# Fused pooled attention and top-1 MoE: two homes for the left operands, one flag for each engine, branches issued ahead of the seven products

## Chip, cores and metric

The kernel runs on one core of a Trainium2 chip. The metric is the device time of one execution in microseconds (us). The engines are TensorE (PE, with its weight loads as PEld), VectorE (DVE), ScalarE (ACT), GpSimd (POOL) and SyncE (SP, which only issues DMAs here).

## What is computed

Attention over keys and values that are averaged in groups of 8, then a mixture of experts in which each of 4608 tokens goes to the one expert with the highest gate.

```python
q, k, v: (8, 8, 576, 64)            # batch, heads, sequence, head size
k_p, v_p = mean of k, v over groups of 8 positions
attn = softmax(q @ k_p.T / 8) @ v_p
x = attn as (4608, 512)             # N tokens, D
logits = x @ w_gate + modality_bias[modality_id]      # 8 experts
e_idx, gate_w = argmax, softmax value there
out[n] = gate_w[n] * (relu(x[n] @ w1[e]) @ w2[e])     # w1: (8, 512, 1024), w2: (8, 1024, 512)
```

## The kernel before

Attention, gating and routing fill the first quarter of the time and are the same in both kernels. Then tokens are sorted by expert into slots of 256 tokens (SLOT). Slots 0 to 17 (NSTAT = 18) always run, one after the other, and the last of them is widened by 128 tokens where that is enough for all. Tokens of one expert fill slots in a row, so that a slot has either the expert of the slot before it or a new one; a flag of 0 or 1 in `meta` says which.

The hidden size of 1024 is worked on in eight blocks f of 128 rows (NF = 8), two blocks making a pair p (0 to 3, with g = 2p). Float32 operands are split in a high and a low part, and each product is made of three: high by high, high by low, low by high. The weights' split parts stand in `hl[f]` (first 512 columns w1, the others w2), each made from a float32 copy `raw[f]`.

For a pair, `hidden_sums` (L195) makes the first products: 24 matmuls (L201) into one PSUM bank `hp`, both chunks (one a block) in the same bank. From slot 3 (FIRST_SEVEN) to slot 16 the second product is done in Strassen's manner, with seven products in place of eight. `first_seven` (L218) applies the relu on ScalarE (L221, L222), VectorE makes sums of the halves (L223 to L225), and `rest` splits them into the left operands `left` (casts on ScalarE, L228 and L230, the low parts on VectorE, L229 and L231). `left` has one home, which every pair overwrites. `seven` (L242) then multiplies, 21 matmuls (L248), with blocks of w2 and with sums of them (`ext[p]`, the "x" pieces) into four PSUM banks that gather over the four pairs. `evac_seven` (L1464) empties these banks at the start of the next slot: ScalarE copies four products with the gate as scale (L1472), GpSimd combines two and two (L1473, L1474), VectorE makes six combinations (L1477), of which products 0 and 1 lie in bank 0.

The order of issue in a slot s is that of `pairs` (L1567), on every engine's queue: for pair 0 the evacuation of the slot before; for pairs 1 to 3 the first products of this pair, the seven products of the pair before, `rest`, `misc`, and `step_done`; at the end, the first products of pair 0 of the next slot, the seven products of pair 3, `rest` and `step_done(4)`. `misc` (L1602) holds the preparation of tokens: gathers, scaling on GpSimd (L326), a write to DRAM (`scr`, L329), a read of it in another order (`y`, L343), transposes on VectorE (L353), and the splits L1399 (ScalarE) and L1404 (VectorE).

`step_done` calls `turn`, which renews the weights for the next slot piece by piece: steps 1 to 4 within slot s, 5 to 7 in the first three steps of slot s + 1. In a step GpSimd makes sums in place in `raw` (SUMS, L253 and L260), ScalarE casts the high parts (L279) and VectorE subtracts for the low parts (L283) of the pieces in PIECES, and SP issues the loads of `raw` of the pairs in FREED for the slot after (L130, L135). Sums and pieces stand in a branch (`changed`, L1496) that is passed over where the expert stays. A branch is issued on all three of ScalarE, VectorE and GpSimd, whichever of them has work in it. For slot 3 the pieces are made without a branch. The last slot but one, 16, has a renewal of its own (`renew_last`, L1507). The only lists that set the order are these:

```python
PIECES = {2: [(0, "e"), (0, "o")], 3: [(1, "e"), (1, "o")], 4: [(0, "x"), (2, "e")], 5: [(2, "o"), (1, "x")],
          6: [(3, "e"), (3, "o"), (2, "x")], 7: [(3, "x")]}
FREED = {4: [0], 5: [1], 6: [2], 7: [3]}
```

## Time and profile before

| | |
|---|---|
| median of 3 runs | 742.31 us (740.21 to 743.71) |
| the profiled execution's own time | 742.09 us |
| its span, first to last instruction | 740.3 us |
| mean granted clock of PE | 0.916 |
| PE busy | 609.7 us, 82% of the span |
| VectorE, GpSimd, ScalarE busy | 446.5 (60%), 311.2 (42%), 306.2 us (41%) |

A slot is told here from the first products of its pair 1 to those of the next slot's. By that, slot 2 goes from 215.74 to 237.93 us, slot 3 to 268.45, slots 4 to 7 to 390.65, 8 and 9 to 465.53, 10 to 12 to 557.62 (11 from 496.33 to 527.10), 13 and 14 to 632.82, 15 to 663.72 and 16 to 696.94. Slots 8, 9, 13 and 14 are those in which pieces are made for a new expert. Busy time of PE is from modelled ends, and a granted clock of 1 is 2.4 GHz, of 0.5 1.2 GHz.

### The profile page before, as it was taken

Reading aid. Unit: us, or ns where it says so; the run is one execution under the profiler, and the core shown is the slowest. Engines: PE = TensorE matmul, PEld = TensorE weight load, DVE = VectorE, ACT = ScalarE, POOL = GpSimd, SP = SyncE. Lnnn points to the kernel's source line nnn. Section 1 sums busy time; section 2 is a strip of 40 time slices with the busy share of each in tenths; the row PEclk is TensorE's granted clock in tenths of the full one; section 3 lists DMA queues with packets and bytes.
Section 4 is the critical chain, followed back from the end, with each engine's and each line's share of the span. In section 5 each row is a group of like instructions: output and inputs, shape, how many; then the busy total and the mean of one; then the engine's idle time right before and its main releaser. Section 6 shows DMA issues by size and latency. Waiting matters only on the chain. (4 is left out here: it accounts for less than half of the span.)

```text
span 740.3 us, 15072 instructions
## 1 busy us (share of the span) xinstructions
PE 609.7 (82%) x4503; PEld 572.8 (77%) x4503; DVE 446.5 (60%) x1009; ACT 306.2 (41%) x702; POOL 311.2 (42%) x438
## 2 busy tenths in 40 slices
PE   5999999999999687786887767786887767885797
PEld 5898999989999687686876767786877757784785
DVE  6878887887665674635536665635536676546321
ACT  3776778963223432432424344422324343423310
POOL 7799686500318623413134644314134655422011
PEclk9999999999999989988989777988989777988889
DMA  9999998431552213112135331112135431223201
GB/s 268 322 291 370 311 336 256 150 111 61 173 171 88 86 44 102 65 53 94 37 101 165 124 111 59 59 59 94 37 101 165 121 93 64 66 86 101 58 31 44
DMA packets 83253, 94.91 MB, mean 128 GB/s; under 512 B 18191, under 2 KB 56591, under 8 KB 83152
## 3 DMA queue, kind: packets, MB, share of 16 engines
q1 hardware_dynamic: 77232, 74.34, 32.3%
q0 software_dynamic: 5920, 19.44, 8.2%
q8 instruction: 37, 0.61, 0.4%
q14 instruction: 64, 0.52, 0.2%
HBM read 113.63 MB, written 28.62 MB: 192 GB/s over the span
## 5 line engine op out<-in xcount | busy, mean ns | idle before, releaser
L201 PE MATMUL hp<-xhl,hl 128*128 128x256 f32 x1536 | 222.3, 304 | 74.0 <-ACTq L1498 44.4
L201 PEld LDWEIGHTS hp<-xhl,hl 128*128 128x128 f32 x1536 | 209.5, 211 | 82.5 <-ACTq L1498 48.8
L248 PE MATMUL op<-hl,after_arow 128*128 128x256 f32 x504 | 83.1, 314 | 26.7 <-DVE ob L1477 26.0
L248 PEld LDWEIGHTS op<-hl,after_arow 128*128 128x128 f32 x504 | 75.6, 222 | 31.1 <-issue 17.3
L223 DVE TENSOR_TENSOR hs<-hs 128x256 f32<-128x256 f32 x56 | 26.5, 473 | 117.6 <-ACT hs L222 116.8
L1473 POOL TENSOR_TENSOR part<-part 128x256 f32<-128x256 f32 x14 | 10.2, 726 | 169.1 <-ACT part L1472 169.1
L221 ACT ACTIVATE hs<-hp 128x256 f32<-128x256 f32 x56 | 21.5, 384 | 142.3 <-PE hp L201 140.8
L231 DVE TENSOR_TENSOR left<-hs,left 128x512 fp32r<-128x512 f32 x56 | 41.4, 738 | 43.2 <-ACT left L230 24.9
L248 PE MATMUL op<-hx,left 128*128 128x256 f32 x378 | 54.8, 291 | 5.4 <-ACT hx L279 4.0
L228 ACT CAST after_arow<-hs 128x384 fp32r<-128x384 f32 x56 | 28.8, 514 | 71.1 <-PE op L248 44.9
L1488 POOL DMA_INDIRECT out_dram<-ob,sidx x28 | 31.9, 1138 | 56.7 <-DMA out_dram<-ob,sidx 29.4
L248 PEld LDWEIGHTS op<-hx,left 128*128 128x128 f32 x378 | 50.8, 202 | 6.1 <-ACT hx L279 4.2
L326 POOL TENSOR_TENSOR xg<-xg 128x256 f32<-128x256 f32 x56 | 47.5, 870 | 17.5 <-DMA xg<-xs,gidx 17.4
L230 ACT CAST left<-hs 128x512 fp32r<-128x512 f32 x56 | 34.7, 620 | 46.3 <-PE op L248 36.6
L792 PE MATMUL av<-vw,pt 128*128 128x146 f32 (+1 forms) x320 | 48.9, 292 | 0.7 <-DVE xb L825 0.6
L148 POOL DMA_INDIRECT xg<-xs,gidx x36 | 38.4, 1067 | 17.6 <-issue 8.0
L792 PEld LDWEIGHTS av<-vw,pt 128*128 128x128 f32 (+1 forms) x320 | 39.6, 180 | 2.5 <-ACT pt L776 0.8
L1477 DVE SCALAR_TENSOR_TENSOR ob<-op,gc,part 128x256 f32<-128x256 f32 x56 | 26.9, 480 | 19.4 <-POOL part L1473 11.9
L229 DVE TENSOR_TENSOR after_arow<-hs,after_arow 128x384 fp32r<-128x384 f32 x56 | 31.6, 565 | 10.3 <-ACT after_arow L228 7.2
L728 PE MATMUL sc<-kt,qt 128*128 128x144 f32 x256 | 37.0, 288 | 0.7 <-ACT qt L709 0.7
L283 DVE TENSOR_TENSOR hl<-raw,hl 128x256 fp32r<-128x256 f32 (+1 forms) x32 | 29.4, 951 | 9.8 <-ACT hl L279 9.3
L728 PEld LDWEIGHTS sc<-kt,qt 128*128 128x128 f32 x256 | 33.2, 190 | 1.2 <-ACT qt L709 0.6
(298 smaller groups left out, 1220.5 us busy)
## 6 DMA issues: line engine op xcount, KB each, us to landing
raw<-in_moe_w_dram SPq DMA_DIRECT2D x248, 256.0 KB
scr<-xg SPq DMA_DIRECT2D x35, 256.0 KB
xs<-xb SPq DMA_DIRECT2D x16, 528.0 KB
k<-in_k_dram SPq DMA_DIRECT2D x7, 1024.0 KB
v<-in_v_dram SPq DMA_DIRECT2D x7, 1024.0 KB
q<-in_q_dram SPq DMA_DIRECT2D x7, 1024.0 KB
y<-scr SPq DMA_DIRECT2D x108, 64.0 KB
v<-in_v_dram SPq DMA_DIRECT2D x16, 128.0 KB
```

What stands on the lines that cost most here:

```text
L148: nc.gpsimd.indirect_dma_start(out=x, out_offset=None, in_=xs[0:rows, :], in_offset=IndirectOffsetOnAxis(idx[:, col:col + 1].bitcast(U32), 0),
L201: nc.tensor.matmul(ph[:, c], hl[g + c][:, w, d * P:(d + 1) * P], ab[:, d, x, 0:SLOT], start=(n == 0 and d == 0), stop=(n == 2 and d == ND ...
L228: nc.scalar.copy(left[0][0], hs[:, 1:4])
L229: nc.vector.tensor_sub(left[0][1], hs[:, 1:4], left[0][0].bitcast(F32))
L230: nc.scalar.copy(left[1][0], hs[:, 4:8])
L231: nc.vector.tensor_sub(left[1][1], hs[:, 4:8], left[1][0].bitcast(F32))
L248: nc.tensor.matmul(at_, left[a][x][:, i], right(p, w, n), start=(p == 0 and k == 0 and n % 2 == 0), stop=(p == NF // 2 - 1 and k == 2 and ...
L283: nc.vector.tensor_sub(lo, src, hi.bitcast(F32))
L326: nc.gpsimd.tensor_tensor(xo, xi, f[:, :, a].to_broadcast([P, ND, 2, QUAD]), op=ALU.mult)
L728: nc.tensor.matmul(dst, qt[:, i, :], kt[b % NB][:, :, h * SPL:(h + 1) * SPL], start=True, stop=True)
L792: nc.tensor.matmul(av[hs, u, 2 * VC * gg:2 * VC * (gg + 1)], pt[:, c, hs], vw[y][:, c].rearrange("p a x -> p (a x)"), start=(gg == 0), sto ...
L1488: nc.gpsimd.indirect_dma_start(out=out[:, :], out_offset=IndirectOffsetOnAxis(idx.bitcast(U32), 0), in_=ob, in_offset=None, bounds_check=N ...
```

## The change

The left operands get a second home (`lefts1`, in the place of a tile that is free in slots 3 to 15), and pairs take turns between the two; so `rest` runs at once after the sums, up to slot 15. In slot 16 there is one home, and `rest` stays behind the seven products. `step_done` is called ahead of the seven products and of `misc`. Each branch is on one engine, with a flag in a register of that engine. The pieces (2, "o"), (3, "e"), (3, "o") and all "x" pieces are made one step earlier, the sums of pairs 2 and 3 likewise, and the loads of `raw` too. The two chunks of a pair lie in two PSUM banks, and pairs take turns between the halves of a bank. The evacuation takes products 0 and 1 first, in VectorE's combinations without GpSimd, whose two instructions come last. Some tiles (`ye`) are used in slots 2 and 3 alone. The diff, without its unchanged lines:

```diff
+ACT, DVE, POOL_ = mybir.EngineType.Activation, mybir.EngineType.DVE, mybir.EngineType.Pool
...
     def hidden_sums(g, ab):
-        ph = hp[(g // 2) % 2].rearrange("p (c t) -> p c t", c=2)
+        h_ = (g // 2) % 2 * SLOT
+        ph = hp2[:, :, h_:h_ + SLOT]
...
-        return lambda: None
-    def first_seven(g, ab):
+    def first_seven(q, g, ab):
...
+        l0, l1 = left[q, g // 2] = lefts[g // 2 % 2 if q < NSTAT - 2 else 0]
...
         def rest():
-            nc.scalar.copy(left[0][0], hs[:, 1:4])
-            nc.vector.tensor_sub(left[0][1], hs[:, 1:4], left[0][0].bitcast(F32))
-            nc.scalar.copy(left[1][0], hs[:, 4:8])
-            nc.vector.tensor_sub(left[1][1], hs[:, 4:8], left[1][0].bitcast(F32))
+            nc.scalar.copy(l0[0], hs[:, 1:4])
+            nc.scalar.copy(l1[0], hs[:, 4:8])
+            nc.vector.tensor_sub(l0[1], hs[:, 1:4], l0[0].bitcast(F32))
+            nc.vector.tensor_sub(l1[1], hs[:, 4:8], l1[0].bitcast(F32))
+        if q < NSTAT - 2:
+            rest()
+            return lambda: None
...
-    def seven(p):
+    def seven(q, p):
...
-                nc.tensor.matmul(at_, left[a][x][:, i], right(p, w, n),
+                nc.tensor.matmul(at_, left[q, p][a][x][:, i], right(p, w, n),
...
-        elif tt == 0 and s <= EARLY_SLOTS:
+        elif tt == 0 and s < FIRST_SEVEN + 1:
...
     def blocks_turn(s, tt):
...
-        elif s <= EARLY_SLOTS:
+        elif s < FIRST_SEVEN + 1:
...
-    hp = [ps_hp.tile([P, 512], F32, name=f"hp{i}") for i in range(2)]
+    hp2 = ps_hp.tile([P, 2, 512], F32, name="hp")
+    hp = [hp2[:, i] for i in range(2)]
...
-    left = [None, second_left[:, 0:8 * P].rearrange("p (z n t) -> p z n t", z=2, n=4)]
-    left[1] = [left[1][:, z] for z in range(2)]
+    lefts, left = [[None, [second_left[:, 4 * P * z:4 * P * (z + 1)].rearrange("p (n t) -> p n t", n=4) for z in range(2)]]], {}
     def take_rows():
...
-        left[0] = [a[:, z] for z in range(2)]
+        lefts[0][0] = [a[:, z] for z in range(2)]
+        b = mp.tile([P, 2 * ND * (SLOT + P)], F32R, tag="xw", name="lefts1")[:, P - 16:]
+        lefts.append([b[:, k * 6 * P:k * 6 * P + 2 * n * P].rearrange("p (z n t) -> p z n t", z=2, n=n) for k, n in ((0, 3), (1, 4))])
+        lefts[1] = [[x[:, z] for z in range(2)] for x in lefts[1]]
...
-    PIECES = {2: [(0, "e"), (0, "o")], 3: [(1, "e"), (1, "o")], 4: [(0, "x"), (2, "e")], 5: [(2, "o"), (1, "x")],
-              6: [(3, "e"), (3, "o"), (2, "x")], 7: [(3, "x")]}
+    PIECES = {2: [(0, "e"), (0, "o")], 3: [(1, "e"), (1, "o"), (0, "x")], 4: [(2, "e"), (2, "o"), (1, "x")],
+              5: [(3, "e"), (3, "o"), (2, "x")], 6: [(3, "x")]}
...
-            4: [(more_sums_of, 1), (sums_of, 3)], 6: [(more_sums_of, 2)], 7: [(more_sums_of, 3)]}
-    FREED = {4: [0], 5: [1], 6: [2], 7: [3]}
+            4: [(more_sums_of, 1), (sums_of, 3)], 5: [(more_sums_of, 2)], 6: [(more_sums_of, 3)]}
+    FREED = {3: [0], 4: [1], 5: [2], 6: [3]}
     def slot_flag(s):
-        flags[s] = nc.values_load(meta[0:1, 2 + NSLOT + s:3 + NSLOT + s],
-                                  engines=[mybir.EngineType.Activation, mybir.EngineType.DVE, mybir.EngineType.Pool], min_val=0, max_val=1,
-                                  skip_runtime_bounds_check_because="a comparison's result")
+        for e in (mybir.EngineType.Activation, mybir.EngineType.DVE, mybir.EngineType.Pool):
+            flags[s, e] = nc.values_load(meta[0:1, 2 + NSLOT + s:3 + NSLOT + s], engines=[e], min_val=0, max_val=1,
+                                         skip_runtime_bounds_check_because="a comparison's result")
     def part(s):
...
-            for n, dst, g in ((1, e2, g0), (2, e5, g1), (4, e6, g0), (5, e7, g1)):
+            low, high = slice(0, H2), slice(H2, D)
+            for n, dst, g in ((2, e5, g1), (1, e2, g0), (4, e6, g0), (5, e7, g1)):
...
-            nc.gpsimd.tensor_sub(e6, e6, e2)
-            nc.gpsimd.tensor_add(e7, e7, e5)
             def combine(out_, n, g, b, minus=False):
...
-            combine(obs[1][:, H2:D], 0, g1, e5)
-            combine(obs[0][:, H2:D], 0, g0, e6)
-            combine(obs[0][:, H2:D], 3, g0, obs[0][:, H2:D])
-            combine(obs[1][:, 0:H2], 6, g1, e7, minus=True)
-            combine(obs[1][:, 0:H2], 3, g1, obs[1][:, 0:H2])
-            combine(obs[0][:, 0:H2], 6, g0, e2)
+            combine(obs[1][:, high], 0, g1, e5)
+            combine(obs[0][:, high], 0, g0, e2, minus=True)
+            combine(obs[0][:, high], 3, g0, obs[0][:, high])
+            combine(obs[1][:, low], 3, g1, e5, minus=True)
+            combine(obs[1][:, low], 6, g1, obs[1][:, low])
+            combine(obs[0][:, low], 6, g0, e2)
+            nc.gpsimd.tensor_add(obs[0][:, high], obs[0][:, high], e6)
+            nc.gpsimd.tensor_sub(obs[1][:, low], obs[1][:, low], e7)
...
-        def changed(fn, q=s + 1):
-            with tc.If(flags[q] > 0, preferred_fallthrough_block=False):
+        def changed(eng, fn, q=s + 1):
+            with tc.If(flags[q, eng] > 0, preferred_fallthrough_block=False):
...
         def renew(f):
...
-                lag.append(lambda: (changed(lambda: split_hi(f)), changed(lambda: split_lo(f, nc.vector))))
+                lag.append(lambda: (changed(ACT, lambda: split_hi(f)), changed(DVE, lambda: split_lo(f, nc.vector))))
         def renew_last(p):
...
-                for do in (halve_hi, halve_lo):
+                for eng, do in ((ACT, halve_hi), (DVE, halve_lo)):
                     def all_of(do=do, part=part):
...
-                        changed(all_of)
+                        changed(eng, all_of)
...
-                work.append(lambda: [fn(p) for fn, p in SUMS[step]])
-            for do in (halve_hi, halve_lo):
+                work.append((POOL_, lambda: [fn(p) for fn, p in SUMS[step]]))
+            for eng, do in ((ACT, halve_hi), (DVE, halve_lo)):
                 def all_of(do=do):
...
-                    work.append(all_of)
-            for fn in work:
+                    work.append((eng, all_of))
+            for eng, fn in work:
...
-                    changed(fn, q + 1)
+                    changed(eng, fn, q + 1)
...
         def step_done(step):
+            if step < 4:
+                turn(s - 1, step + 4)
...
-            if step < 4:
-                turn(s - 1, step + 4)
+            elif step > 1:
+                renew_last(step - 2)
             if s == FIRST_SEVEN - 2:
...
         def first_of(q, g):
-            return (first_seven if FIRST_SEVEN <= q < NSTAT - 1 else first_pair)(g, tokens_of(q))
+            if FIRST_SEVEN <= q < NSTAT - 1:
+                return first_seven(q, g, tokens_of(q))
+            first_pair(g, tokens_of(q))
+            return lambda: None
         def second_pair(p):
...
-                seven(p)
+                seven(s, p)
...
                 if g:
...
+                    step_done(g // 2)
...
-                        seven(g // 2 - 1)
+                        seven(s, g // 2 - 1)
...
-                    if s == NSTAT - 2:
-                        renew_last(g // 2 - 1)
-                    step_done(g // 2)
...
-                    if s == NSTAT - 2:
-                        xw[0] = mp.tile([P, ND, 2, SLOT + P], F32R, tag="xw", name="xw")
...
+                    if s == NSTAT - 2:
+                        xw[0] = mp.tile([P, ND, 2, SLOT + P], F32R, tag="xw", name="xw")
...
+                step_done(4)
...
-                step_done(4)
         def misc(f, later):
...
         def close(first_of_next=first_next):
...
-                seven(NF // 2 - 1)
+                renew_last(NF // 2 - 2)
+                seven(s, NF // 2 - 1)
...
```

## Rows read from the trace of the kernel before

**Rows 1.** Busy time of each engine by stretches (us from the span's start): slot 2, slot 3, slots 4 to 7, 8 and 9, 10 to 12, 11 alone, 13 and 14, 15, 16. Behind each engine's busy time stand its instructions; PEclk is the granted clock.

```profile
215.74:237.93 22.19, 22.19 (x148) 20.31 (x146) 10.65 (x22) 5.31 (x12) 16.94 (x22) 1.00 0.30 98
237.93:268.45 30.52, 24.41 (x181) 23.55 (x180) 21.06 (x46) 13.15 (x27) 13.76 (x14) 0.89 0.22 70
268.45:390.65 122.20, 95.86 (x722) 92.05 (x721) 61.76 (x142) 39.52 (x88) 36.97 (x40) 0.92 0.22 71
390.65:465.53 74.88, 54.48 (x363) 52.36 (x361) 47.86 (x77) 30.27 (x56) 38.37 (x40) 0.82 0.36 113
465.53:557.62 92.09, 73.55 (x543) 70.75 (x541) 44.78 (x97) 29.65 (x66) 27.22 (x30) 0.89 0.22 70
496.33:527.10 30.77, 24.75 (x182) 23.81 (x181) 14.93 (x33) 9.88 (x22) 9.00 (x10) 0.89 0.22 70
557.62:632.82 75.20, 53.90 (x363) 51.81 (x361) 48.80 (x77) 30.37 (x56) 38.20 (x40) 0.82 0.36 111
632.82:663.72 30.90, 24.35 (x183) 23.41 (x181) 15.39 (x33) 9.88 (x22) 11.20 (x13) 0.89 0.27 87
663.72:696.94 33.22, 23.39 (x171) 22.33 (x169) 16.73 (x39) 11.64 (x27) 4.66 (x5) 0.90 0.28 79
```

In each row: stretch, its length, then PE, PEld, DVE, ACT, POOL, the granted clock, the DMA engines' share and GB/s.

**Rows 2.** PE's timeline in slot 11: start, time, instructions in a row, and in brackets the idle time before them and what ended it.

```profile
500.30 0.93 PE L248 MATMUL op<-hl,after_arow 128*128 128x256 f32 x6 [0.97 <-DVE ob L1477]
501.73 0.59 PE L248 MATMUL op<-hl,after_arow 128*128 128x256 f32 x3 [0.51 <-DVE ob L1477]
...
506.41 1.63 PE L201 MATMUL hp<-xhl,hl 128*128 128x256 f32 x12 [1.31 <-ACTq L1498]
...
512.33 1.21 PE L201 MATMUL hp<-xhl,hl 128*128 128x256 f32 x8 [1.91 <-ACTq L1498]
514.86 3.78 PE L201 MATMUL hp<-xhl,hl 128*128 128x256 f32 x16 [1.32 <-DVEq L1498]
...
521.80 2.99 PE L201 MATMUL hp<-xhl,hl 128*128 128x256 f32 x24
524.63 1.23 PE L248 MATMUL op<-hl,after_arow 128*128 128x256 f32 x9
...
527.10 2.89 PE L201 MATMUL hp<-xhl,hl 128*128 128x256 f32 x24
```

**Rows 3.** The view of waits over the whole run: who waited for whom, us in total, times, the longest. ACTq and DVEq L1498 are the branches on those engines.

```profile
ACT after_arow L228 <- PE op L248: 44.9, 25, 4.2
PE hp L201 <- ACTq L1498: 44.4, 22, 4.7
ACT left L230 <- PE op L248: 36.6, 43, 2.1
PE op L248 <- DVE ob L1477: 26.0, 24, 4.9
PE hp L201 <- DVEq L1498: 16.1, 10, 2.1
PE hp L201 <- ACT hl L279: 10.3, 4, 3.3
```

**Rows 4.** The timeline of VectorE and of ScalarE in slot 11 (columns as in rows 2), VectorE first.

```profile
499.67 0.48 DVE L1477 SCALAR_TENSOR_TENSOR ob<-op,gc,part 128x256 f32<-128x256 f32 x1 [0.76 <-POOL part L1473]
...
511.04 1.14 DVE L231 TENSOR_TENSOR left<-hs,left 128x512 fp32r<-128x512 f32 x1 [0.59 <-ACT left L230]
...
512.77 1.03 DVE L1404 TENSOR_TENSOR xhl<-yt,xhl 128x512 fp32r<-128x512 f32 x1
...
526.20 0.28 DVE L225 TENSOR_TENSOR hs<-hs 128x128 f32<-128x128 f32 x1
527.88 0.69 DVE L231 TENSOR_TENSOR left<-hs,left 128x512 fp32r<-128x512 f32 x1 [0.74 <-ACTq L1498]
...
497.56 1.57 ACT L1472 ACTIVATE part<-op,gc 128x256 f32<-128x256 f32 x4 [0.48 <-ACTq L1498]
...
510.39 0.62 ACT L230 CAST left<-hs 128x512 fp32r<-128x512 f32 x1 [0.53 <-PE op L248]
...
524.83 0.39 ACT L221 ACTIVATE hs<-hp 128x256 f32<-128x256 f32 x1 [2.28 <-PE hp L201]
```

**Rows 5.** Groups of instructions by line and shape in slots 8 and 9: count, busy us and mean ns of one, idle time before them and what ended it.

```profile
L283 DVE TENSOR_TENSOR hl<-raw,hl 128x1024 fp32r<-128x1024 f32 x8 | 10.7, 1369 | 2.5 <-ACT hl L279 2.4 <-issue 0.2
L279 ACT CAST hl<-raw 128x1024 fp32r<-128x1024 f32 x8 | 8.1, 1042 | 1.1 <-issue 1.1
L256 POOL TENSOR_TENSOR raw<-raw,raw 128x256 f32<-128x256 f32 x4 | 4.5, 1132 | 6.9 <-DMA raw<-in_moe_w_dram 6.9
L263 POOL TENSOR_TENSOR raw<-raw,raw 128x256 f32<-128x256 f32 x4 | 3.7, 922 | 6.6 <-DVE hl L283 4.2 <-issue 1.4 <-DMA scr<-xg 1.0
L283 DVE TENSOR_TENSOR hx<-raw,hx 128x768 fp32r<-128x768 f32 x3 | 3.4, 1133 | 0.1
L279 ACT CAST hx<-raw 128x768 fp32r<-128x768 f32 x3 | 2.5, 828 | 0.0
```

**Rows 6.** PE's timeline in slot 9: the seven products of pair 0, with the idle time before them.

```profile
433.17 2.41 PE L248 MATMUL op<-hl,after_arow 128*128 128x256 f32 x9 [4.61 <-DVE ob L1477]
```

**Rows 7.** The branches' line: engine, instruction, count, shortest, median and longest ns, first and last start.

```profile
L1498 ACTq COMPARE_BRANCH  x448: 34/38/50, 246.2 to 700.2; - x150
```

**Rows 8.** SP's timeline in slot 11: the eight reads of y, from the first issue to the end of the last.

```profile
516.42 3.67 SPq L343 DMA_DIRECT2D y<-scr  x8
```

## The prediction, made before the changed kernel was run

> **What bounds the kernel now.** I read the stretches first, one slot each [rows 1]. Slot 2, still with plain second products, is the measure: 22.19 us long, PE busy for 22.19 of them, clock 1.00. Every slot with seven products should be shorter, as four block pairs of 24 + 21 matmuls are 180. In slot 11 the undisturbed part shows their price: 24 first products take 2.83 us from start to start (521.80 to 524.63), 21 of the seven products 2.47 (524.63 to 527.10) [rows 2]. A step is 5.30 us, a slot 21.2. It takes 30.77, with PE at a granted clock of 0.89 [rows 1].
>
> The same timeline says where the 9.6 us go [rows 2]. PE stands for 0.97 + 0.51 us ahead of the first seven products (released by the evacuation's combinations, L1477), 1.31 in the middle of pair 2's first products (ScalarE's branch), and 1.91 + 1.32 in pair 3's (ScalarE's branch, then VectorE's): 6.0 us. After these the same 16 matmuls take 3.78 us, and a clock of 0.89 loses 0.11 x 30.77 = 3.4 us. 21.2 + 6.0 + 3.4 = 30.6. So each such slot is PE's own work plus waits plus the half clock that follows the waits. The view of waits has the same order for the whole run: branches on ScalarE 44.4 us, evacuation 26.0, branches on VectorE 16.1, weight casts 10.3 [rows 3].
>
> Why the branches are late is in the two vector engines' timeline [rows 4]. Issue order puts them behind the casts of the left operands and behind `misc`. The casts L228 and L230 wait for PE to finish reading the one home that the left operands have (44.9 and 36.6 us in all [rows 3]): L230 starts at 510.39, VectorE's L231 at 511.04, and L1404 runs until 513.80. Only then does VectorE pass the branch that frees the lower halves of the weights, and PE goes on at 514.86 [rows 2].
>
> **Part by part.** Eight slots change no expert (4 to 7, 10 to 12, 15): 122.20 + 92.09 + 30.90 = 245.2 us. Two pairs of slots carry an expert change: 74.88 and 75.20. Slot 3 takes 30.52 and slot 16 33.22 [rows 1].
>
> *Branches ahead, two homes.* In the new order a pair's relus, sums and casts follow its first products at once, then the branches, and `misc` last. With two homes the casts wait for the seven products of two pairs ago, which are done. From the end of the first products (524.79) to the end of L225 is 1.7 us; L230 adds 0.6, L231 0.7: 3.0 us, or 3.5 where L231 takes 1.14 beside GpSimd [rows 4]. Its seven products start 2.47 + 2.83 = 5.30 us after that end. The branches come 0.3 to 0.6 us later, and what they guard is read a step or more later still, as pieces (2, "o"), (3, "e"), (3, "o") are one step earlier than before. So the 1.31 + 1.91 + 1.32 us cost nothing any more; the cover is 2 us, and beyond it each us is PE's.
>
> What is late next on VectorE: behind the branches stand two transposes, or two L1404 (2.1 us), or the evacuation's six combinations (2.9). 3.3 + 2.9 us exceeds a step by 0.9, which the next chain's 2 us absorb. VectorE's work in a slot is 14.93 us [rows 1], 70% of 21.2.
>
> *Evacuation in bank order.* Today bank 0 is free after three copies, a GpSimd subtraction and the second combination, which ends at 500.15 with 0.76 us waiting on GpSimd [rows 4]; PE starts at 500.30. New: two copies and two combinations, nothing of GpSimd between. ScalarE is through its casts and branch 1.7 + 0.6 + 0.3 = 2.6 us after the last first products; four copies take 1.57, so bank 0 is free at 2.6 + 0.8 + 1.0 = 4.4 of 5.30. GpSimd's two additions move behind the combinations; only the row writes wait for them.
>
> *Two PSUM banks for a pair.* L221 starts at 524.83, when all 24 matmuls have ended, though its chunk was ready 12 matmuls (1.4 us) before [rows 2, 4]. That was one bank; now it may start with the first chunk. L222 still waits for the last matmul, so the chain gains 0.3 us of which nothing lies on the path. The Trainium skill ("PSUM — Partial Sum Buffer", PSUM bank collisions) has engines kept apart by bank and not by address, and the late L221 agrees. That speaks against the change: the next pair's chunk now shares a bank with this pair's, and its first matmul must wait for L221 and L222. By the rows the wait is nothing while relus start within 2.47 us, and about 0.9 us for each expert change, where ScalarE is late.
>
> *A flag per engine.* 448 compares on each of three engines [rows 7] are two for each branch, 16 branches a slot. Five remain on ScalarE and VectorE, six on GpSimd. Three in a row cost ScalarE 0.48 us ahead of the copies [rows 4]; none of that is PE's, so I count it at nothing beyond the cover above.
>
> *Weight loads a step earlier, on SP.* Four loads a step now stand ahead of the eight reads of y (3.67 us [rows 8]), and wait for VectorE to pass step 3's branch, about 17 us into the slot. The reads are then issued by 23 us, and the transposes want y at 27.5: hidden, with 4.5 us left for the landing, whose length no row here shows.
>
> *Slots with an expert change.* Here VectorE has 47.86 us of work [rows 1] against 42.4 of PE. Per step 2 casts of 1.04 and one of 0.83 on ScalarE, 2 x 1.37 + 1.13 = 3.9 us on VectorE, and on GpSimd two sums of 1.1 and three of 0.9 [rows 5]. The "x" pieces are cast in the same step that makes their sums, so ScalarE waits for GpSimd with the next relus behind it. Laid out from the start of the first slot: step 3's sums end at 21.6, ScalarE's third cast at 22.5, pair 0's left operand at 26.3 instead of 21.9. Step 4's pieces stand ahead of the evacuation: casts until 28.6, copies until 29.4, VectorE's pieces until 30.7, two combinations: bank 0 free at 31.7, wanted at 24.7. That is 7 us, where now it is 4.61 [rows 6]. The waits after it add 4, the clock 4: 42.4 + 15 is 57.4, taken as 58, against 75.
>
> *Slots 3 and 16.* Slot 3 loses the long waits for its "x" pieces, and keeps one of about 1.2: 23. Slot 16 keeps one home, but its casts no longer hold back branches: 180 matmuls less what the wider last product costs are 20.5, with 3 of waits 23.5; the evacuation after it gains some 2.
>
> **Sum**, on the profiled execution's 742.09 us (the median is 742.31):
> - eight slots, 0.8 us each kept for what I don't see: 8 x 22.0 = 176; -69
> - two expert changes: 2 x 58 = 116 for 150.1; -34
> - slot 3: -7.5; slot 16 and what follows: -12
>
> -122.5, so 619.6: I say 620. Bounds: all waits and half clocks gone (-76 -52 -9 -14) is 591; a kept evacuation wait with its half clock (26 us a slot, -36), and -10, -3, -5 for the rest, is 688.
>
> **Rivals.**
> 1. *VectorE becomes the bound.* L231 takes 1.14 instead of 0.69 us beside GpSimd [rows 4], and shorter slots put more of GpSimd's 9.00 us [rows 1] beside VectorE. If all of it held VectorE up, 14.93 + 9.00 = 23.9 us; with the wait and a half clock that this brings, 26 a slot: -37, expert changes at 64 (-22), -10 for the rest: 673. For it: VectorE is in order, and its margin is 2 us. Against it: slots 1 and 2 run without a gap. The Trainium skill ("SBUF — State Buffer", SBUF: two separate sides) calls the shared port pair an exclusive lock for a VectorE instruction with two SBUF inputs; the 1.14 us agrees in kind, and by that rule the full 9 us could count.
> 2. *The change doesn't free PE from the branches*: the wait that PE makes is met only behind some later piece of the same engine, so the three waits stay and only the evacuation and the left operands gain. 1.5 us and some clock, 2.5 a slot: 742 - 20 - 7 = 715. Against it: the waits name the branch, and the branch moves.
> 3. *Slower: SP brings y late.* The reads of y stand behind loads that wait for VectorE; late y stops the transposes on VectorE, and with them the next left operands. It costs nothing until y comes 4.5 us after the last read's issue; it undoes the gain where a slot grows by 9.4 us, so at about 14 us; at 15 the slots take 31 to 32 and the time is about 750. SP's queue is otherwise half empty, so I see nothing that makes 14.
>
> **How the numbers follow.** Forecast (600 to 645) 0.62; VectorE bound (645 to 690) 0.22; branches still waited for (690 to 735) 0.08; no change 0.03; SP 0.05. 0.5% (3.7 us) is what a measurement of this kernel tells from no change. Leaving out 2 in 10 gives 600 to 675. Faster 0.92, same 0.03, slower 0.05.
>
> **What would show it.** Slots 5 and 11 at 21 to 23 us with clock 1.00 and no idle on L201; VectorE at 70% of them; casts L228 and L230 released by VectorE and not by PE; no wait on L1473 in the evacuation; 7 us ahead of the first seven products after each expert change. I'm wrong if PE still idles over 1 us in an undisturbed slot, if the clock still falls there, or if L353 waits for y.

## The result, and the profile after

After the change the kernel takes 643.87 us (median of 4 runs, 642.13 to 645.64), before 741.26 (739.73 to 743.71) in the same comparison: ratio 0.8684, 95% interval 0.8647 to 0.8721. The prediction was 620, range 600 to 675: the direction is right, the point 24 us too low, and the experiments take away one of its reasons.

The stretches after, one row a slot or a run of slots; columns as in [rows 1]. The rows are slots 4 to 7, slot 8, slot 9, slot 11, slot 14 and slot 16:

```profile
core 0: us, PE busy (x) PEld busy (x) DVE busy (x) ACT busy (x) POOL busy (x), PEclk, DMA share, GB/s
263.65:354.13 90.48, 86.82 (x722) 84.51 (x721) 64.72 (x142) 40.04 (x89) 37.22 (x40) 1.00 0.30 96
354.13:383.80 29.67, 24.16 (x182) 23.64 (x181) 22.31 (x33) 13.78 (x26) 18.79 (x19) 0.88 0.66 214
383.80:421.66 37.86, 26.51 (x182) 25.66 (x181) 29.42 (x46) 16.78 (x31) 19.30 (x22) 0.77 0.20 64
442.69:465.45 22.76, 21.82 (x183) 21.10 (x181) 15.79 (x32) 9.77 (x22) 9.12 (x10) 1.00 0.29 95
517.48:555.29 37.81, 25.17 (x183) 24.39 (x181) 30.18 (x45) 16.69 (x31) 20.39 (x22) 0.86 0.18 57
576.91:602.43 25.52, 22.64 (x170) 21.99 (x169) 17.55 (x41) 11.33 (x28) 4.67 (x6) 0.93 0.49 146
```

The unchanged slots run at clock 1.00; slot 11 went from 30.77 to 22.76 us. The slots with an expert change (8 and 9, 13 and 14) are where the time stays: 67.5 and 68.2 us, clock 0.77 to 0.89. PE's waits in the whole run, columns as in [rows 3]:

```profile
PE op L253 <- DVE ob L1484: 15.7, 3, 8.1
PE hp L203 <- DVE xhl L1412: 15.2, 6, 6.7
PE hp L203 <- ACT hs L224: 6.5, 5, 1.9
```

The branches, 44.4 and 16.1 us in [rows 3], are gone from the list. The wait for a relu (L224) is new: in the kernel before no first product waits for one. In slot 11 PE's timeline, beside [rows 2], has two short stops left:

```profile
453.71 2.90 PE L203 MATMUL hp<-xhl,hl 128*128 128x256 f32 x24
...
459.96 2.55 PE L203 MATMUL hp<-xhl,hl 128*128 128x256 f32 x20 [0.49 <-DVE xhl L1412]
...
463.10 1.10 PE L253 MATMUL op<-hl,lefts 128*128 128x256 f32 x7 [0.37 <-DVE lefts L232]
```

(L203 is the first products, L253 the seven products, L223 and L224 the relus, L230 and L231 the casts of left operands, L232 and L233 their low parts, L284 and L288 the pieces' casts and subtractions, L261 to L270 GpSimd's sums, L149 the gathers, L331 the scaling, L1412 the low half of the token split, L1481 and L1484 the evacuation's copies and combinations, L1497 the row writes, L1507 the branches.) ScalarE and VectorE in the same slot, to be set beside [rows 4]:

```profile
456.64 0.38 ACT L223 ACTIVATE hs<-hp 128x256 f32<-128x256 f32 x1 [0.82 <-PE hp L203]
461.66 0.51 ACT L230 CAST lefts<-hs 128x384 fp32r<-128x384 f32 x1 [4.35 <-DVE hs L225]
458.69 0.15 DVE L314 COPY gc<-xg 128x1 f32<-128x1 f32 x1 [1.92 <-DMA xg<-xs,gidx]
460.68 0.15 DVE L314 COPY gc<-xg 128x1 f32<-128x1 f32 x1 [0.78 <-DMA xg<-xs,gidx]
```

The left casts wait for VectorE's sums and no longer for PE. What stops VectorE is L314: a copy of the gate column out of gathered rows, which waits for the gather with the token split and the next pair's sums behind it. In the kernel before, this copy waited 0.2 us in the whole run; now it waits 29.3 us, 19 times.

In the expert change PE stops here, slots 8 and 9 on PE's timeline:

```profile
376.42 4.63 PE L203 MATMUL hp<-xhl,hl 128*128 128x256 f32 x20 [5.51 <-DVE xhl L1412]
394.12 2.26 PE L253 MATMUL op<-hl,after_arow 128*128 128x256 f32 x9 [7.42 <-DVE ob L1484]
405.18 2.99 PE L203 MATMUL hp<-xhl,hl 128*128 128x256 f32 x24 [1.06 <-ACT hs L224]
412.46 1.11 PE L203 MATMUL hp<-xhl,hl 128*128 128x256 f32 x4 [1.90 <-ACT hs L224]
414.54 4.64 PE L203 MATMUL hp<-xhl,hl 128*128 128x256 f32 x20 [0.97 <-DVE gc L314]
```

7.42 + 1.06 + 1.90 + 0.97 are forecast (7 and 4). The 5.51 us in slot 8 are not. (Slots 13 and 14 have 6.65 us in this place, then 8.11 and 4.54.) GpSimd's timeline of slot 8 shows what is ahead of the first pair's last sums (L268 to L270):

```profile
361.99 1.32 POOL L1497 DMA_INDIRECT out_dram<-ob,sidx  x1 [0.15 <-POOL raw L262]
367.55 1.00 POOL L1497 DMA_INDIRECT out_dram<-ob,sidx  x1 [4.25 <-DMA out_dram<-ob,sidx]
368.86 1.83 POOL L149 DMA_INDIRECT xg<-xs,gidx  x1 [0.30 <-issue]
371.00 1.40 POOL L149 DMA_INDIRECT xg<-xs,gidx  x1 [0.31 <-issue]
...
375.20 3.15 POOL L331 TENSOR_TENSOR xg<-xg 128x256 f32<-128x256 f32 x4 [1.38 <-DMA xg<-xs,gidx]
...
380.07 1.19 POOL L270 TENSOR_TENSOR raw<-raw,raw 128x256 f32<-128x256 f32 x1
381.21 1.73 POOL L261 TENSOR_TENSOR raw<-raw,raw 128x256 f32<-128x256 f32 x1
```

Two row writes with 4.25 us between them for the first one's landing, two gathers, 1.38 us for a gather's landing, 3.15 us of scaling. The sums end at 381.26, 27.1 us into the slot; the prediction laid them out to 21.6. The same gather stops VectorE ahead of the token split that PE's 5.51 us name:

```profile
375.16 0.15 DVE L314 COPY gc<-xg 128x1 f32<-128x1 f32 x1 [3.65 <-DMA xg<-xs,gidx]
375.23 1.14 DVE L1412 TENSOR_TENSOR xhl<-yt,xhl 128x512 fp32r<-128x512 f32 x1
```

### The profile page after: what moved, and what is told of

Read it like the earlier page. It is cut to its first block, busy times and chain, and to the rows that moved or that the text cites. A ratio compares the mean times of both kernels' runs of the same rounds, so it can differ in the third digit from the quotient of the medians.

```text
span 643.9 us, 14102 instructions
## 1 busy us (share of the span) xinstructions
PE 576.1 (89%) x4503; PEld 543.5 (84%) x4503; DVE 457.8 (71%) x1009; ACT 306.1 (48%) x702; POOL 311.5 (48%) x438
## 5 line engine op out<-in xcount | busy, mean ns | idle before, releaser
L203 PE MATMUL hp<-xhl,hl 128*128 128x256 f32 x1536 | 200.1, 287 | 25.0 <-DVE xhl L1412 15.2
L203 PEld LDWEIGHTS hp<-xhl,hl 128*128 128x128 f32 x1536 | 191.7, 196 | 29.4 <-DVE xhl L1412 17.9
L1497 POOL DMA_INDIRECT out_dram<-ob,sidx x28 | 29.9, 1068 | 60.0 <-DMA out_dram<-ob,sidx 38.7
L253 PE MATMUL op<-hl,after_arow 128*128 128x256 f32 x270 | 41.5, 297 | 17.9 <-DVE ob L1484 15.7
L253 PEld LDWEIGHTS op<-hl,after_arow 128*128 128x128 f32 x270 | 36.4, 199 | 21.2 <-ACT hs L224 17.8
L331 POOL TENSOR_TENSOR xg<-xg 128x256 f32<-128x256 f32 x56 | 45.7, 843 | 14.1 <-DMA xg<-xs,gidx 13.0
L149 POOL DMA_INDIRECT xg<-xs,gidx x36 | 42.3, 1176 | 17.6 <-issue 8.0
L797 PE MATMUL av<-vw,pt 128*128 128x146 f32 (+1 forms) x320 | 48.9, 292 | 0.9 <-DVE xb L830 0.8
L230 ACT CAST lefts<-hs 128x384 fp32r<-128x384 f32 x26 | 13.3, 513 | 76.1 <-DVE hs L225 76.1
L253 PE MATMUL op<-hl,lefts 128*128 128x256 f32 x312 | 46.7, 283 | 1.2 <-DVE lefts L232 1.2
L253 PEld LDWEIGHTS op<-hl,lefts 128*128 128x128 f32 x312 | 41.4, 192 | 2.0 <-DVE lefts L232 1.8
L253 PE MATMUL op<-hx,left 128*128 128x256 f32 x261 | 36.7, 287 | 0.0
L223 ACT ACTIVATE hs<-hp 128x256 f32<-128x256 f32 x56 | 21.4, 381 | 28.6 <-PE hp L203 25.7
L253 PEld LDWEIGHTS op<-hx,left 128*128 128x128 f32 x261 | 34.1, 197 | 0.0
L1407 ACT CAST xhl<-yt 128x512 fp32r<-128x512 f32 x26 | 16.1, 620 | 34.1 <-DVE yt L358 28.8
L740 DVE TENSOR_REDUCE mx<-sc 128x8 f32<-128x576 f32 (+1 forms) x40 | 27.7, 691 | 5.6 <-PE sc L733 5.0
L801 PE MATMUL av<-vw,pt 128*128 128x146 f32 (+1 forms) x160 | 30.3, 292 | 0.8 <-ACT pt L781 0.6
```

What stands on the lines that cost most here:

```text
L149: nc.gpsimd.indirect_dma_start(out=x, out_offset=None, in_=xs[0:rows, :], in_offset=IndirectOffsetOnAxis(idx[:, col:col + 1].bitcast(U32), 0),
L203: nc.tensor.matmul(ph[:, c], hl[g + c][:, w, d * P:(d + 1) * P], ab[:, d, x, 0:SLOT], start=(n == 0 and d == 0), stop=(n == 2 and d == ND ...
L223: nc.scalar.activation(hs[:, 0:2], ph[:, 0].rearrange("p (t x) -> p t x", t=2), AF.Relu)
L253: nc.tensor.matmul(at_, left[q, p][a][x][:, i], right(p, w, n), start=(p == 0 and k == 0 and n % 2 == 0), stop=(p == NF // 2 - 1 and k == ...
L331: nc.gpsimd.tensor_tensor(xo, xi, f[:, :, a].to_broadcast([P, ND, 2, QUAD]), op=ALU.mult)
L740: nc.vector.reduce_max(mx, scv, axis=AX.X)
```

## Experiments

One table first. Slot lengths in us from the traces (from one slot's first products of pair 1 to the next slot's): the mean of the eight unchanged slots, slots 8 + 13, slots 9 + 14, slot 3. The ratio is to the kernel before on the same chip.

| kernel | median us | ratio, 95% interval | unchanged | 8 + 13 | 9 + 14 | 3 |
|---|---|---|---|---|---|---|
| before | 741.3 | | 30.65 | 70.5 | 79.6 | 30.5 |
| after | 643.9 | 0.868 (0.865–0.872) | 22.19 | 60.0 | 75.7 | 24.3 |
| e_gate | 630.6 | 0.850 (0.846–0.854) | 21.07 | 57.6 | 73.9 | 24.2 |
| e_gather | 638.6 | 0.859 (0.856–0.863) | 21.28 | 59.9 | 74.2 | 29.7 |
| e_evac_first | 647.4 | 0.873 (0.868–0.878) | 22.34 | 60.7 | 76.7 | 24.3 |
| e_gate_evac | 629.2 | 0.847 (0.843–0.851) | 21.02 | 58.1 | 75.1 | 24.2 |
| e_gate_x | 621.2 | 0.838 (0.835–0.841) | 21.37 | 46.7 | 72.7 | 24.4 |
| e_gate_old | 638.8 | 0.860 (0.857–0.864) | 22.11 | 46.4 | 84.8 | 24.9 |
| e_gate_nosums | 600.5 | 0.809 (0.806–0.812) | 21.00 | 42.1 | 59.9 | 24.3 |
| u_behind | 639.6 | 0.863 (0.859–0.867) | 21.18 | 61.0 | 74.0 | 28.3 |
| u_home_behind | 644.5 | 0.865 (0.861–0.869) | 21.33 | 65.4 | 72.2 | 28.7 |
| u_flag | 650.3 | 0.873 (0.868–0.877) | 22.58 | 58.5 | 78.1 | 24.6 |
| u_evac | 635.4 | 0.854 (0.849–0.858) | 22.25 | 57.1 | 68.4 | 24.1 |
| u_lists_behind | 688.6 | 0.929 (0.923–0.934) | 26.94 | 63.1 | 68.2 | 29.0 |

Five of the twelve times lie in a range that was given for them. Seven lie outside all of theirs, three of these by under 0.5 us (e_evac_first, u_behind, u_flag).

### Why the expert changes cost 68 us and not 58

Theory A: the stops are L314's waits and step 4's pieces ahead of the evacuation. Theory B: VectorE has more work in these slots than they hold. **e_gate** copies the gate columns two steps later, when the gathers have landed; **e_gather** issues the gathers ahead of the row writes; **e_evac_first** puts the whole of step 4, GpSimd's sums as well as the pieces, behind the evacuation; **e_gate_evac** is the first and the third together.

```
e_gate, out of blocks_out into blocks_in:
+        if tt < 2 and s > 1:
+            keep_gate(s, tt, nc.vector)
e_gather, in misc: the gather(s + 2, xg) block ahead of
             if f == 2:
                 while later: later.pop(0)()
e_evac_first (pending is run behind the evacuation):
-                step_done(4)
+                if s >= FIRST_SEVEN:
+                    pending.append(lambda: step_done(4))
```

Expected of e_gate: 

> The changed kernel with one edit: VectorE's copy of the gate column (L314) is issued two steps later, beside the read of y, and no longer ahead of the second split of the tokens (L1412). Theory A: in the first slot of each expert change PE's 5.5 us wait (released by L1412) is VectorE waiting in that copy for a gather that GpSimd issues late; with the copy moved the wait goes, and the half clock behind it: 2 x (5.5 + 3) = 17 us less, about 627 (622 to 633), slots 8 and 13 at 21.5 to 24. Theory B: VectorE has too much work at an expert change, and what it doesn't wait for in the copy it waits for elsewhere: 639 or more, slots 8 and 13 at 28 or more.

Expected of e_gather: 

> The changed kernel with one edit: GpSimd issues the two gathers of a slot ahead of the two row writes, of which the second waits for the first to land (4.25 us in slot 8). Theory A (the gather is late because of that wait): the copy of the gate no longer waits, as with the copy moved, 2 x (5.5 + 3) less, 627 to 633. If the gather is late because the weight loads slow its own transfer, the wait stays: 640 to 644. Theory B (VectorE's work is the bound): 639 or more.

Expected of e_evac_first: 

> The changed kernel with one edit: from slot 3 on the branches of step 4 are issued behind the evacuation in the next slot, not ahead of it. Theory A: the 7.4 us that PE stands ahead of the first seven products after an expert change are step 4's pieces on ScalarE (2.8 us) and VectorE (3.3 us) and GpSimd's sums, standing ahead of the evacuation; behind it they cost PE little: 2 x (5 + 2 of clock) = 14 less, about 630 (626 to 636), slots 9 and 14 at 30 to 33. Theory B: VectorE is the bound in these slots, and the order of its work changes nothing: 640 to 647.

Expected of e_gate_evac: 

> Both edits of e_gate and e_evac_first. Theory A: their gains add, 643.9 - 17 - 14 = 613 (606 to 620), with the four slots of the expert changes together at 105 us in place of 135.7. Theory B: VectorE's 52 us of work in two slots plus the waits of an in-order queue keep them at 125 or more: 633 or more.

e_gate met A's time, but not at A's place. Five unchanged slots came to 20.84 us, while slot 8 lost only 0.9 us and kept a gap of 6 us, one pair further on, with another releaser. e_gather shortened the unchanged slots alone, and lengthened slot 3, where PE then waited 5.61 us for slot 2's evacuation; in its slot 8 L314 no longer waits, and PE stops 7.50 us for a relu. e_evac_first gained nothing: its slots 9 and 14 are no shorter than those of the changed kernel, and e_gate_evac's no shorter than e_gate's. Yet the wait that A named there is gone: in slot 9 of e_gate_evac PE doesn't stop ahead of the first seven products. It stops ahead of the next pair's first products, for a relu behind an x piece that waits for a sum:

```profile
387.09 5.49 PE L203 MATMUL hp<-xhl,hl 128*128 128x256 f32 x24 [4.75 <-ACT hs L224]
385.65 0.83 ACT L284 CAST hx<-raw 128x768 fp32r<-128x768 f32 x1 [4.84 <-POOL raw L270]
```

The edit had moved the sums back together with the pieces, so it doesn't test the place of the pieces alone. So L314 is what the unchanged slots still waited for, and at the expert changes A falls: without the stops that it named, others of the same size stand. In e_gate these are the rows of PE and of the two engines behind it (lines past L337 stand 2 later than in the changed kernel):

```profile
375.71 2.50 PE L203 MATMUL hp<-xhl,hl 128*128 128x256 f32 x10 [6.07 <-ACT hs L224]
374.27 0.83 ACT L284 CAST hx<-raw 128x768 fp32r<-128x768 f32 x1 [5.18 <-POOL raw L270]
375.28 0.38 ACT L224 ACTIVATE hs<-hp 128x256 f32<-128x256 f32 x1
367.51 4.56 POOL L331 TENSOR_TENSOR xg<-xg 128x256 f32<-128x256 f32 x4 [1.86 <-DMA xg<-xs,gidx]
373.51 0.72 POOL L270 TENSOR_TENSOR raw<-raw,raw 128x256 f32<-128x256 f32 x1
```

PE waits for the relu L224; the relu stands on ScalarE behind the x piece; the x piece waits 5.18 us for GpSimd's sum L270; the sum stands behind the scaling. That is theory C, against B, that VectorE simply has too much work. **e_gate_x** moves the x pieces and the loads that wait for them back to the steps of the kernel before; **e_gate_old** takes the whole old list; **e_gate_nosums** leaves the sums out.

```
e_gate_x:
-    PIECES = {2: [(0, "e"), (0, "o")], 3: [(1, "e"), (1, "o"), (0, "x")], 4: [(2, "e"), (2, "o"), (1, "x")],
-              5: [(3, "e"), (3, "o"), (2, "x")], 6: [(3, "x")]}
-    FREED = {3: [0], 4: [1], 5: [2], 6: [3]}
+    PIECES = {2: [(0, "e"), (0, "o")], 3: [(1, "e"), (1, "o")], 4: [(2, "e"), (2, "o"), (0, "x")],
+              5: [(3, "e"), (3, "o"), (1, "x")], 6: [(2, "x")], 7: [(3, "x")]}
+    FREED = {4: [0], 5: [1], 6: [2], 7: [3]}
e_gate_nosums:
-            if step in SUMS:
+            if step in SUMS and forced:
```

Expected of e_gate_x: 

> The kernel e_gate with the x pieces of pairs 0 to 3 one step later (steps 4 to 7, the steps of the kernel before) and the weight loads of a freed pair at steps 4 to 7 too; nothing is left out. Theory C (GpSimd's sums come late: row writes, gathers and 4.6 us of scaling stand ahead of them, ScalarE waits in order for the x piece, 5.2 us at 374.3 in e_gate, and the relu behind it releases the 6.07 us gap at 375.71 and the 1.70 us one at 403.5): slots 8 and 13 fall from 28.8 to 22.5 to 24, slots 9 and 14 from 36.3 and 37.6 to 33 to 35; 610 to 619, I say 615. Theory B (VectorE has more work than a step holds in the slots with an expert change): the two slots together stay at 63 to 67 us, 626 to 633.

Expected of e_gate_old: 

> The kernel e_gate with the whole list of pieces of the kernel before (steps 2 to 7: 2, 2, 2, 2, 3 and 1 pieces) and the weight loads at steps 4 to 7, but the sums as in the changed kernel; nothing is left out. Theory C: as for the x pieces alone, and step 4, ahead of the evacuation, has two pieces instead of three, so the 4.87 us gap ahead of slot 9's first seven products falls to about 3: 605 to 616, I say 611. Theory B: the work is only spread over other steps, 626 to 633. Against both: the pieces (2, o), (3, e) and (3, o) come a step later and PE could wait for them as in the kernel before, 1.3 us and some half clock in each slot: 635 or more.

Expected of e_gate_nosums: 

> The kernel e_gate with GpSimd's sums of the weights left out in slots 8, 9, 13 and 14 (the seven products there take unsummed weights); the casts and subtractions of the x pieces stay. Theory C: no piece waits for a sum, and VectorE's chain of 4.9 us beside GpSimd (377.2 to 382 in e_gate) falls to the 2.4 us that it takes alone: slots 8 and 13 at 22 to 24, slots 9 and 14 at 30 to 34, 600 to 614, I say 607. Theory B with VectorE's own instructions as the bound: the gaps stay within 3 us of a slot pair, 624 to 631.

(In e_gate_old the pieces (3, "e") are cast in the step whose sums overwrite half of them first, so some weights differ; the work is that of its lists.) Slots 8 and 13 fell by 11 us together in e_gate_x, as C says, and the time by 9.4 us. Slots 9 and 14 hardly moved: the stop ahead of slot 9's first seven products grew from 4.87 us in e_gate to 10.03. It is the one long wait left there; PE, and VectorE ahead of it:

```profile
383.97 2.26 PE L253 MATMUL op<-hl,after_arow 128*128 128x256 f32 x9 [10.03 <-DVE ob L1486]
378.25 3.40 DVE L288 TENSOR_TENSOR hl<-raw,hl 128x1024 fp32r<-128x1024 f32 x2 [0.62 <-POOL raw L262]
381.56 1.47 DVE L288 TENSOR_TENSOR hx<-raw,hx 128x768 fp32r<-128x768 f32 x1
382.96 0.86 DVE L1486 SCALAR_TENSOR_TENSOR ob<-op,gc,part 128x256 f32<-128x256 f32 x2
```

Step 4's pieces, ahead of the evacuation, still wait for a sum and run beside GpSimd. With the sums left out the first slot of a change is an unchanged slot and the second loses 7 us (slots 8 and 9):

```profile
345.31:366.33 21.02, 20.95 (x183) 20.71 (x181) 17.35 (x30) 13.27 (x26) 7.63 (x8) 1.00 0.80 253
366.33:396.33 30.00, 23.71 (x182) 23.54 (x181) 26.91 (x47) 16.67 (x31) 13.63 (x13) 0.89 0.27 88
```

So GpSimd's sums, by coming late and by lengthening VectorE's instructions, cost 30 us of e_gate's 630.6; how the two share it, no run shows. B may keep the rest, though no run moved the pieces without the sums: in slot 9 of e_gate_nosums the gap ahead of the first seven products remains, with the pieces ahead of the evacuation:

```profile
375.70 1.62 PE L253 MATMUL op<-hl,after_arow 128*128 128x256 f32 x6 [6.29 <-DVE ob L1486]
```

e_gate_old shows the other side of the list: with "o" and "e" of the last pairs a step later, PE waited 8.76 us in slot 9 for the cast of a piece (L284), and slots 9 and 14 grew to 84.8. In its unchanged slots PE waits again for ScalarE's branches, up to 1.4 us each.

### Which part freed the unchanged slots

Five kernels undo parts of the change.

```
u_behind, in pairs (and the same at the slot's end):
                     do_late(s, g)
-                    step_done(g // 2)
 ...
                     misc(g + 1, later)
+                    step_done(g // 2)
u_home_behind, with that:
-        l0, l1 = left[q, g // 2] = lefts[g // 2 % 2 if q < NSTAT - 2 else 0]
+        l0, l1 = left[q, g // 2] = lefts[0]
 ...
-        if q < NSTAT - 2:
-            rest()
-            return lambda: None
         return rest
u_flag: one values_load for the three engines
u_evac: the combinations of the kernel before, GpSimd's two first
u_lists_behind: u_behind, and PIECES, SUMS, FREED of the kernel before, with its order of the two turns in step_done
```

Expected of u_behind: 

> The changed kernel with the branches and pieces put back behind the seven products and behind the gathers, transposes and splits (the order of the kernel before), all else of the change kept. My prediction's step (the branches' place is what PE waits for: 1.31 + 1.91 + 1.32 us and the half clock that follows): these waits come back in the eight unchanged slots, 4 to 8 us each, 680 to 715. Rival (the one home for left operands made the branches late; with two homes they pass in time from the old place): the unchanged slots stay at 21 to 23.5 us, 640 to 660.

Expected of u_home_behind: 

> The changed kernel with one home for the left operands, as before, and the branches behind the seven products, as before; flags per engine, lists of pieces, evacuation and PSUM as in the changed kernel. With the branches behind alone the time was 639.6, the unchanged slots at 20.84. Theory H (one home makes the casts wait for PE, and the branches behind them come late; either two homes or branches ahead is enough): the waits in pairs 2 and 3 come back, unchanged slots 25 to 29, 675 to 710. Rival F (the branches that an engine passed for the others were the delay): 638 to 650, unchanged slots at 20.8 to 22.5.

Expected of u_flag: 

> The changed kernel with each flag again one value for three engines, so that ScalarE, VectorE and GpSimd each pass every one of the 16 branches of a slot (448 compares each, as before, for 128 and 144); all else of the change kept. My prediction's step (counted at nothing beyond the cover of 2 us): 640 to 650. Rival F (the branches of the other engines' work are what was late: three in a row cost ScalarE 0.48 us ahead of its copies before, and PE waited for branches in 44 + 16 us of the run): waits for ScalarE's and VectorE's branches come back, unchanged slots 24 to 29 us, 665 to 705.

Expected of u_evac: 

> The changed kernel with the evacuation of the seven products in its old order (GpSimd's subtraction and addition ahead of the combinations); all else of the change kept. My prediction's step (the old order frees bank 0 0.9 to 1.5 us later than PE wants it, and half clock follows): unchanged slots 23.5 to 26 instead of 22.2, 655 to 675. Rival (with two homes the copies start early enough, and the old order fits too): 642 to 650.

Expected of u_lists_behind: 

> The changed kernel with two parts undone together: the lists of pieces, sums and freed pairs of the kernel before, and the branches behind the seven products and what follows them, as before. Two homes, the new evacuation, the flags per engine and the PSUM layout stay; nothing is left out. Each part alone cost the unchanged slots nothing to 1 us (20.84 us with the branches behind, 21.7 to 22.0 with the old list of pieces). Theory L (PE waits where a piece's branch comes both late in its step and only one step ahead of its reader; the earlier list or the place ahead is enough): the waits of 1 to 2 us in pairs 2 and 3 and the half clock come back, unchanged slots 25 to 30, 670 to 710, I say 690. Rival H (it takes the one home as well, since the casts that waited for PE were what made the branches late): unchanged slots 20.8 to 23, 630 to 655.

The rival had u_behind's slots right: with the branches back behind everything the unchanged slots are at 21.18 us, shorter than after. Its reason, the second home, falls, and theory H with it: in u_home_behind, with one home as well, they are at 21.33. F falls too: three-engine flags cost 0.4 us a slot, not 2 to 7, and as their ratio's interval overlaps that of after, I call even that not shown. Only u_lists_behind brings the old waits back, 688.6 against the 690 of theory L. Its waits of PE over the whole run, and slot 11 on PE's timeline:

```profile
PE hp L203 <- ACTq L1507: 37.8, 22, 4.3
PE hp L203 <- DVEq L1507: 16.1, 10, 3.0
```

```profile
473.38 1.65 PE L203 MATMUL hp<-xhl,hl 128*128 128x256 f32 x12 [1.57 <-ACTq L1507]
...
478.46 1.20 PE L203 MATMUL hp<-xhl,hl 128*128 128x256 f32 x8 [1.05 <-ACTq L1507]
481.15 3.56 PE L203 MATMUL hp<-xhl,hl 128*128 128x256 f32 x16 [1.49 <-DVEq L1507]
```

These are the 1.31, 1.91 and 1.32 us of [rows 2], at the same three places and with the two homes in place. Pieces a step earlier, or branches ahead of the seven products: either takes these waits away or nearly so. u_behind has the first alone. The nearest run to the second alone is e_gate_old, with the old pieces but the new sums and the copy out of the way: 22.11 us, 1.0 more than e_gate. Both undone cost 215.5 - 177.5 = 38 us of the 67.7 that the eight slots gained. The other 30 belong to the homes, the evacuation, the flags and the PSUM layout together; how they share it was not tried.

u_evac shows a trade. PE and VectorE in its slot 11:

```profile
439.37 0.95 PE L253 MATMUL op<-hl,after_arow 128*128 128x256 f32 x6 [0.27 <-DVE ob L1485]
440.87 0.58 PE L253 MATMUL op<-hl,after_arow 128*128 128x256 f32 x3 [0.55 <-DVE ob L1485]
438.74 0.48 DVE L1485 SCALAR_TENSOR_TENSOR ob<-op,gc,part 128x256 f32<-128x256 f32 x1 [0.76 <-POOL part L1481]
```

The old order does make VectorE wait 0.76 us for GpSimd and PE 0.8 us for VectorE in each unchanged slot, as [rows 4] had it, but no half clock follows: its unchanged slots run at 1.00. They are no longer than the changed kernel's (22.25 and 22.19 us), as L314 waits 5.0 us in this run and not 29.3. And u_evac as a whole is faster than both forecasts for it and than the changed kernel; 7.3 us of that are its shorter slots 9 and 14. GpSimd's row writes of slot 9, in the changed kernel (slot from 383.80) and in u_evac (from 380.76):

```profile
400.04 1.05 POOL L1497 DMA_INDIRECT out_dram<-ob,sidx  x1 [1.14 <-DVE lefts L233]
404.13 0.99 POOL L1497 DMA_INDIRECT out_dram<-ob,sidx  x1 [3.04 <-DMA out_dram<-ob,sidx]
```

```profile
394.83 1.22 POOL L1496 DMA_INDIRECT out_dram<-ob,sidx  x1 [1.13 <-DVE hs L227]
398.06 1.37 POOL L1496 DMA_INDIRECT out_dram<-ob,sidx  x1 [2.02 <-DMA out_dram<-ob,sidx]
```

The second stands 20.3 us into the slot in the one and 17.3 in the other. In the new order GpSimd's two additions are last and wait for VectorE's combinations, so its writes and the sums behind them come 2 to 3 us later. In the changed kernel ScalarE's last x piece waits for these sums, and PE waits 1.90 us for the relu behind it:

```profile
410.13 0.83 ACT L284 CAST after_arow<-raw 128x768 fp32r<-128x768 f32 x1 [3.30 <-POOL raw L270]
```

Neither this stop nor the 1.06 us one, whose relu stands behind VectorE's transposes, is in u_evac's slot 9. They are 3.0 of the 4.9 us by which that slot is shorter.

e_gate_x, at 621.2 us, is the fastest kernel here that computes the whole result.

## Why the prediction was right or wrong

**Eight slots, 176 for 177.5 measured.** The term holds, and most signs it named came: no idle on a branch, left casts released by VectorE, clock 1.00, VectorE at 69% of slot 11. One sign of being wrong came too: in slot 4 PE idles 2.22 us on L203, released by L314. A slot is 22.19 us, and 20.84 where nothing stops PE (forecast 21.2); of the 1.35 between them e_gate took away 1.12, so what the 0.8 us kept for the unseen stood for was mostly L314. That the term came so near is in part luck: 21.2 was 0.36 too high and 0.8 was 0.55 too low. But the reason given was one of several. "Branches ahead, two homes" credited the place of the branches and the homes; u_behind and u_home_behind undo both, and the unchanged slots lose nothing. The clause on pieces one step earlier was there, as an aside to why a late branch doesn't hurt; it was, beside the place, the other of two causes of which one is enough, or nearly so.

**Evacuation.** Bank 0 in time in an unchanged slot: right, of the waits on it one of 0.20 us remains, in slot 4. u_evac shows the stop that it saves, 0.8 us a slot, not the 1.48 us with a half clock that stood in [rows 2]. "Only the row writes wait" for GpSimd's moved additions missed what is queued behind them on GpSimd: the gathers that L314 waits for, and the sums, 7.3 us in slots 9 and 14.

**Expert changes, 116 for 135.7 measured.** This is most of the miss: 19.7 of the 26 us between 619.6 and the profiled execution's 645.64. The step that failed is the layout's first line, "step 3's sums end at 21.6": they end at 27.1. It gave GpSimd only its sums, and left out what stands ahead of them in its queue in that slot, row writes that wait for one another's landing, gathers and scaling: 361.99 to 378.35, 16.4 us, of which two sums are 1.4. In the changed kernel the 5.51 us gap comes from the gathers of that queue: late behind the second row write, they stopped VectorE at L314 for 3.65 us. With the copy out of the way (e_gate) the late sums kept a gap of the same size, one pair further on. The half clock was forecast at 4 us a change: PE is busy for 50.7 us in slots 8 and 9, where two slots without a stop have 2 x 20.84 = 41.7, so it cost 9.0 (7.2 in 13 and 14). The later waits came out at their size, 7.42 us for 7 and others of 3.9 for 4, but the 7 is in part luck: bank 0 was wanted at 32.6 and free at 40.0 us into the slot, not at 24.7 and 31.7, and both ends moved by the same 8 us.

**Slots 3 and 16.** 24.3 for 23 and 25.5 for 23.5; what follows gained 1.9 for 2. Slot 3 starts at 239.35 us, before at 237.93; for these 1.4 us I found no cause in the change.

**Two PSUM banks.** "Now it may start with the first chunk" did not happen: L223 starts at 456.64, after all 24 first products (453.71 + 2.90), and none of the 56 in the run starts earlier. What the prediction held against the layout did happen, and was sized too low: first products that wait for the relus of the pair before, which lies in the same two banks. It said 0.9 us for each expert change; PE's waits for L224 are 6.5 us in the changed kernel, 6.2 of them in the two changes, 17.8 in e_gate and 31.0 in e_gate_evac, and none in the kernel before. So theory C's chain, from a late sum to PE, runs through this layout. The layout was not undone by itself; whether PE would then have stopped a step later, at the left operands, stays open.

**Rivals.** VectorE as the bound of an unchanged slot fell (20.84 us in e_gate); in the second slot of a change it is part of the bound. Branches still waited for: fell, but u_lists_behind is that case at 688.6. SP with y late: the transposes (L358) wait for y nowhere.

## What to carry to other kernels

When a change has several parts that push the same wait out of the way, each may be enough: undo them in pairs before one gets the credit. Before a step is counted as hidden, lay out the whole in-order queue of the engine that does it, with its DMA issues and the landings that they wait for; the cheapest fixes here were moving a one-column copy and a cast a step away from what they waited for.

## What the runs showed of the hardware

VectorE's instructions with two SBUF inputs lengthen beside GpSimd's, in both directions. L232 in slot 9 of e_gate, beside the sums, and in e_gate_nosums:

```profile
378.83 1.09 DVE L232 TENSOR_TENSOR after_arow<-hs,after_arow 128x384 fp32r<-128x384 f32 x1
```

```profile
369.78 0.55 DVE L232 TENSOR_TENSOR after_arow<-hs,after_arow 128x384 fp32r<-128x384 f32 x1
```

In the changed kernel GpSimd's L261 took 0.73 to 0.84 us in three of its four places in slots 8 and 9 and 1.73 at 381.21, where VectorE ran a piece's subtraction. The Trainium skill ("SBUF — State Buffer", SBUF: two separate sides) calls the shared port pair an exclusive lock, in which the one that comes second is blocked for the other's whole instruction. The 0.54 us that L232 gains, less than one sum, agrees with that; no run here tells it from a shared bandwidth.
